# Two of the four steps that decode a 64-bit weight are rewritten from 16-bit halves to 32-bit words

## The chip, the cores and the metric

One core of one Trainium2 chip runs the kernel. The metric is the device time of one execution in microseconds. The runs of the kernel before took 761.26, 761.75 and 769.0 us, median 761.75 us.

## The reference

Three stages follow each other; the inputs of the first are float32, the weights of the other two are float64.

- Attention with a small state: x is (4, 8, 512, 64), state is (4, 8, 32, 64). `softmax(x·stateT/8)·state` gives 512 rows per batch and head, `softmax(state·xT/8)·x` gives 32 more. The result is 4·544 = 2176 tokens of 512 features.
- First MLP: `softplus(tokens @ w_in) @ w_out`, with moe_w_in 512×2048 and moe_w_out 2048×512. The weights are float64, the result is rounded to float32.
- Second MLP, with moe2_w_in, moe2_w_out (float64) and moe2_alpha: `h = x @ w_in`, `g = max(h, 0) + alpha·min(h, 0)`, `g @ w_out`, for the 2176 tokens. Digits are left out of names in the profile, so that moe_w_in stands for both MLPs' w_in.

## The kernel before, in words

**Weights.** Each of the eight quarter groups (four of each MLP, numbered g = 0 to 7) needs four chunks of w_in and four of w_out. A chunk is 128 partitions × 512 numbers of 64 bits, 512 KB. `weight_chunk` handles one: a DMA on SP's queue brings it into a staging tile (`st`, two slots in rotation; two chunks at the very start go to `stx`), seen there as 32-bit words at a step of two (8 bytes) or as 16-bit halves at a step of four. The 64-bit float is turned into a 32-bit float in four steps, all in place:

1. L268, ACT: the low word's upper half holds the bits of which three have to be moved up. A scale and a bias turn it into an integer 0 to 7, written to the low word's lower half (16 bits read, 16 bits written).
2. L270, ACT: the high word, read as a float32, times 2^-112, which leaves the exponent and mantissa bits where the shift below needs them.
3. L271, DVE: the sign bit of the high word (its upper half and 0x8000) is written to the low word's upper half.
4. L275, DVE: high word shifted left by three, or'ed with the low word. This is the float32 weight.

Then `split` (L216 on ACT, L217 on DVE) writes it as a rounded high part and a remainder, the two operands of TensorE's three passes. The remainder's subtraction is what sets the staging slot free for the next load.

**TensorE's work.** For the first 140 us or so the attention of the four batches, the products of state and w_in (`m`), and the first units of the first MLP run side by side; afterwards the work is almost only 128×512 matmuls (L226) of the two MLPs, with ACT and DVE doing the activation, the splits and the accumulation in SBUF.

**Order.** Nothing runs in the order in which it is written. Every operation is added to a graph with an engine, a price in us and the keys that it reads and writes (`G.add`). `order` then works back from the end to give each operation a due time, plays the graph forward with the prices, and emits every engine's instructions in the order that comes out. On the chip each engine runs its list in that order, and waits where the next instruction's inputs are not there. The prices of ACT are `act_us` (0.154 us + 0.714 ns per element from SBUF), those of DVE `dve_us` (0.069 us + one element per cycle of 0.96 GHz; with its second argument true, two). L268 and L270 are priced alike, L271 at the faster of DVE's rates. Where an operation's key was read or written by an earlier one, it waits for that; L271 writes the half that L268 reads, and reads the word that L270 writes.

Of the kernel before, what the change touches and what calls it, by code (L numbers as in the profile page):

```python
# [14 lines left out]
AF = mybir.ActivationFunctionType  # L15
ALU = mybir.AluOpType
# [25 lines left out]
PE, ACT, DVE, SP = "PE", "ACT", "DVE", "SP"  # L42
# [113 lines left out]
def act_us(n, psum):  # L156
    return n * 0.000714 + (0.112 if psum else 0.154)


def dve_us(n, fast=False):  # L160
    return n / (1920.0 if fast else 960.0) + 0.069
# [3 lines left out]
def attention_then_mlps_kernel(ctx: ExitStack, tc: tile.TileContext, xT, xn, st, st0, w1i, w1o, w2i, w2o, alpha, out):  # L165
    nc = tc.nc
    V, A, T = nc.vector, nc.scalar, nc.tensor
    G = Graph()
# [12 lines left out]
    def part(tag, name, dtype=F32, n=2048):  # L181
        if name not in lazy:
            lazy[name] = sb.tile([P, n], dtype, tag=tag, name=name)
        return lazy[name]
# [19 lines left out]
    def ring(name, n):  # L204
        count[name] = count.get(name, -1) + 1
        return count[name] % n
# [7 lines left out]
    def split(hi, lo, src, n, r, w, psum=False, also=()):  # L214
        k = [x + ("hi",) for x in w]
        G.add(ACT, act_us(n, psum), lambda: A.activation(now(hi), now(src), AF.Copy), r, k + [x for x in also if x not in k])  # L216
        G.add(DVE, dve_us(n), lambda: V.tensor_tensor(out=now(lo), in0=now(src), in1=now(hi), op=ALU.subtract), list(r) + k, [x + ("lo",) for x in w])  # L217
# [15 lines left out]
    def load(dst, src, w, r=(), nbytes=0):  # L233
        G.add(SP, 0.06, lambda: nc.sync.dma_start(out=now(dst), in_=now(src)), r, w, delay=2.4 + nbytes / RATE)
# [3 lines left out]
    def wi_ap(g, j):  # L238
        return WI[g % 2][j]().rearrange("p (c f) -> p c f", f=FW)

    def wo_ap(g, j):
        return WO[g % 2][j].rearrange("p (c d) -> p c d", d=DM)
# [4 lines left out]
    def wf(c):  # L247
        return WF()[:, c * FW:(c + 1) * FW]

    def weight_chunk(g):  # L250
        c = chunk[g]
        chunk[g] += 1
        gl = g % NG
        w_in, w_out = (w1i, w1o) if g < NG else (w2i, w2o)
        if c < KC:
            src, dst, key = w_in[c * P:(c + 1) * P, gl * FW:(gl + 1) * FW], [lambda j=j, c=c: wi_ap(g, j)[:, c, :] for j in range(2)], ("wi", g % 2, c)
        else:
            c -= KC
            src, dst, key = w_out[(gl * FC + c) * P:(gl * FC + c + 1) * P, :], [wo_ap(g, j)[:, c, :] for j in range(2)], ("wo", g % 2, c)
        extra = chunk[g] - 1 if g == 0 and chunk[g] > NST and chunk[g] <= KC else None  # L260
        i = ring("st", NST) if extra is None else None
        t = lambda: STG[i] if extra is None else part("m2", "stx", I64, 1024)[:, (extra - NST) * 512:(extra - NST + 1) * 512]
        floats = lambda: t().bitcast(F32).rearrange("p (f t) -> p f t", t=2)[:, :, 1]
        words = lambda: t().bitcast(U32).rearrange("p (f t) -> p f t", t=2)
        halves = lambda: t().bitcast(U16).rearrange("p (f t) -> p f t", t=4)
        q = lambda k: ("st", i, k) if extra is None else ("m", 2, extra - NST, k // 2, ("hi", "lo")[k % 2])
        load(t, src, [q(0), q(1), q(2), q(3)], nbytes=P * 4096)
        G.add(ACT, act_us(512, False), lambda: A.activation(halves()[:, :, 0], halves()[:, :, 1], AF.Copy, scale=2.0 ** -13, bias=2.0 ** -14 - 0.5),  # L268
              [q(1)], [q(0)])
        G.add(ACT, act_us(512, False), lambda: A.activation(floats(), floats(), AF.Copy, scale=2.0 ** -112), [], [q(2), q(3)])  # L270
        G.add(DVE, dve_us(512, True), lambda: V.tensor_scalar(out=halves()[:, :, 1], in0=halves()[:, :, 3], scalar1=0x8000, scalar2=None, op0=ALU.bitwise_and),  # L271
              [q(3)], [q(1)])
        whole = g == 0 and key[0] == "wi"
        fk = ("wi", 1, c, "hi")
        G.add(DVE, dve_us(512), lambda: V.scalar_tensor_tensor(out=wf(c).bitcast(U32) if whole else words()[:, :, 1], in0=words()[:, :, 1], scalar=3, in1=words()[:, :, 0],  # L275
                                                              op0=ALU.logical_shift_left, op1=ALU.bitwise_or),
              [q(0), q(1), q(2), q(3)], [fk] if whole else [q(2), q(3)])
        if whole:
            first_in.append(lambda: split(dst[0], dst[1], lambda: wf(c), 512, [fk], [key]))
        else:  # L280
            split(dst[0], dst[1], floats, 512, [q(2), q(3)], [key],
                  also=[("wi", 1, x, "hi") for x in range(KC)] if key[:2] == ("wi", 1) and g == 1 else [])
# [409 lines left out]
    def run(plan):  # L692
        units = [c for c in plan.split() if c[0] == "u"]
        n = -1
        for c in plan.split():
            if c[0] == "w":
                weight_chunk(int(c[1]))
            elif c == "m00":
                make_first_m()
            elif c[0] == "q":  # L700
                load_first(int(c[1]))
            elif c[0] == "v":
                first_in.pop(0)()
            elif c[0] == "m":
                make_m(int(c[1]), int(c[2]), "d" in c)
            elif c[0] == "t":
                load_state(int(c[1]))
            elif c[0] == "p":
                split_state(int(c[1]))
            elif c[0] == "X":  # L710
                split_x2(int(c[1]))
            elif c[0] == "n":
                load(nalpha, alpha.rearrange("(c p) -> p c", p=P), [("nalpha",)])
                G.add(DVE, 0.07, lambda: V.tensor_scalar(out=nalpha, in0=nalpha, scalar1=-1.0, scalar2=None, op0=ALU.mult), [], [("nalpha",)])
            elif c[0] == "S":
                step_s(int(c[1]))
                flush(LAG)
            elif c[0] == "u":
                b, g, fc = (int(x) for x in c[1:])
                n += 1  # L720
                step1(g, b, fc, n < FC or units[n - FC][1] != c[1], n + FC >= len(units) or units[n + FC][1] != c[1])
                flush(LAG)
            else:
                parts[int(c[1])][c[0]]()
# [4 lines left out]
    for g in range(NG, 2 * NG):  # L729
        for i in range(len(tiles)):  # L730
            for fc in range(FC):
                step2(g, i, fc)
                flush(LAG)
                if g == NG and i == 0 and fc == FC - 1:
                    for k in range(2, len(tiles)):
                        split_x2(k)
                if g + 1 < 2 * NG and i > 0 and chunk[g + 1] < 2 * KC:
                    weight_chunk(g + 1)
# [41 lines left out]
```

## Time and profile before

| | |
|---|---|
| runs | 761.26, 761.75, 769.0 us |
| profiled execution | 771.34 us, of which the span from first to last instruction is 768.5 us |
| mean granted TensorE clock | 0.987 of full |
| busy: PE, ACT, DVE | 747.2, 441.7, 415.5 us (97%, 57%, 54%) |
| L268 on ACT | 64 instructions (62 on `st`, 2 on `stx`), 84.8 us for the 62 |
| L271 on DVE | 64 instructions, 46.8 us for the 62 |

PE, PEld, ACT, DVE and SP are the five queues that the profile speaks of: matmuls, weight loads into the array, ScalarE, VectorE and the DMA issues. PE's busy share is high because matmuls are pipelined and their ends are modelled; what counts here is where it is idle. A duration is that of one instruction from start to end; on ACT the next instruction may start a little before the one ahead has ended.

### The profile page before, as it was taken

Reading aid. Unit: us, or ns where it says so; the run is one execution under the profiler, and the core shown is the slowest. Engines: PE = TensorE matmul, PEld = TensorE weight load, DVE = VectorE, ACT = ScalarE, POOL = GpSimd, SP = SyncE. Lnnn points to the kernel's source line nnn. Section 1 sums busy time; section 2 is a strip of 40 time slices with the busy share of each in tenths; the row PEclk is TensorE's granted clock in tenths of the full one; section 3 lists DMA queues with packets and bytes.
Section 4 is the critical chain, followed back from the end, with each engine's and each line's share of the span. In section 5 each row is a group of like instructions: output and inputs, shape, how many; then the busy total and the mean of one; then the engine's idle time right before and its main releaser. Section 6 shows DMA issues by size and latency. Waiting matters only on the chain.

```text
span 768.5 us, 9148 instructions
## 1 busy us (share of the span) xinstructions
PE 747.2 (97%) x3528; PEld 621.1 (81%) x3528; DVE 415.5 (54%) x693; ACT 441.7 (57%) x739; POOL 0.7 (0%) x6
## 2 busy tenths in 40 slices
PE   7988999999999999999999999999999999999996
PEld 6676788888788888888888898888988889888895
DVE  4786766666746753666682223764347643333342
ACT  5798989786646653766574435873347533333331
POOL 0000000000000000000000000000000000000000
PEclk8899999999999999999999999999999999999999
DMA  8334331136234513341120001220012000001111
GB/s 328 110 110 139 113 131 56 55 123 179 75 91 110 139 51 75 107 123 56 32 77 2 1 0 29 89 103 0 1 56 82 28 1 1 0 1 56 55 56 68
DMA packets 20383, 55.90 MB, mean 73 GB/s; under 512 B 4084, under 2 KB 4084, under 8 KB 19828
## 3 DMA queue, kind: packets, MB, share of 16 engines
q1 hardware_dynamic: 20340, 55.33, 22.9%
q8 instruction: 27, 0.44, 0.2%
q14 instruction: 16, 0.13, 0.1%
HBM read 43.00 MB, written 4.46 MB: 62 GB/s over the span
## 4 chain that ended last, share of the span: by engine, by line
PE 84%; ACT 8%; DMA 3%; DVE 3%; issue 1%; SPq 0%; ACTq 0%; DVEq 0%
PE pa L226 43%; PE ph L226 35%; PE px L226 3%; ACT st L268 3%; DMA st<-in_moe_w_in 2%; PE pa L348 1%; ACT st L270 1%; ACT xf L395 1%; PE ph L485 1%; DVE st L271 0%; ACT L501 0%; PE px L429 0%; ACT m L216 0%; DMA st<-in_moe_w_out 0%; ACT gs L216 0%
## 5 line engine op out<-in xcount | busy, mean ns | idle before, releaser
L226 PE MATMUL pa<-wo,gs 128*128 128x512 f32 x816 | 198.4, 390 | 0.0
L226 PE MATMUL pa<-gs,wo 128*128 128x512 f32 x768 | 191.6, 393 | 0.2 <-DVE xf L523 0.2
L226 PEld LDWEIGHTS pa<-wo,gs 128*128 128x128 f32 x816 | 152.1, 188 | 30.5
L226 PEld LDWEIGHTS pa<-gs,wo 128*128 128x128 f32 x768 | 143.1, 188 | 32.0 <-DVE xf L523 1.3
L226 PE MATMUL ph<-at,wi 128*128 128x512 f32 (+1 forms) x512 | 151.7, 377 | 0.0
L507 ACT ACTIVATE e<-ph 128x512 f32<-128x512 f32 (+2 forms) x80 | 42.7, 533 | 133.1 <-PE ph L226 132.9
L509 DVE SCALAR_TENSOR_TENSOR g<-u,nalpha,e 128x512 f32<-128x512 f32 (+2 forms) x80 | 53.5, 669 | 113.2 <-ACT u L508 113.1
L226 PEld LDWEIGHTS ph<-at,wi 128*128 128x128 f32 x512 | 95.5, 188 | 16.8
L226 PE MATMUL ph<-at,m 128*128 128x512 f32 x384 | 100.4, 397 | 0.5 <-ACT e L501 0.5
L268 ACT ACTIVATE st<-st 128x512 uint16<-128x512 uint16 x62 | 84.8, 1368 | 25.1 <-DMA st<-in_moe_w_in 20.2
L217 DVE TENSOR_TENSOR gs<-g,gs 128x512 fp32r<-128x512 f32 (+2 forms) x101 | 63.3, 627 | 62.5 <-ACT gs L216 48.3
L216 ACT ACTIVATE gs<-g 128x512 fp32r<-128x512 f32 (+2 forms) x101 | 59.0, 584 | 54.1 <-DVE g L509 46.4
L523 DVE TENSOR_TENSOR xf<-pa,xf 128x512 f32<-128x512 f32 x99 | 65.3, 688 | 39.0 <-PE pa L226 38.9
L226 PEld LDWEIGHTS ph<-at,m 128*128 128x128 f32 x384 | 72.3, 190 | 16.8 <-ACT e L501 1.0
L271 DVE TENSOR_SCALAR st<-st 128x512 uint16<-128x512 uint16 x62 | 46.8, 755 | 53.8 <-ACT st L270 53.7
L226 PE MATMUL ph<-m,wi 128*128 128x512 f32 (+1 forms) x192 | 71.8, 374 | 0.0
L270 ACT ACTIVATE st<-st 128x512 f32<-128x512 f32 x62 | 43.7, 704 | 0.0
L275 DVE SCALAR_TENSOR_TENSOR st<-st 128x512 uint32<-128x512 uint32 x60 | 41.5, 692 | 1.6
L508 ACT ACTIVATE u<-ph 128x512 f32<-128x512 f32 (+2 forms) x80 | 42.3, 529 | 0.0
L226 PEld LDWEIGHTS ph<-m,wi 128*128 128x128 f32 x192 | 36.0, 188 | 5.7
L216 ACT ACTIVATE wo<-st 128x512 fp32r<-128x512 f32 x32 | 21.5, 670 | 18.2 <-DVE st L275 11.1
L217 DVE TENSOR_TENSOR wo<-st,wo 128x512 fp32r<-128x512 f32 x32 | 22.1, 693 | 16.2 <-ACT wo L216 15.2
(116 smaller groups left out, 660.7 us busy)
## 6 DMA issues: line engine op xcount, KB each, us to landing
st<-in_moe_w_out SPq DMA_DIRECT2D x32, 512.0 KB, 3.3
st<-in_moe_w_in SPq DMA_DIRECT2D x30, 512.0 KB, 4.4
m<-mt SPq DMA_DIRECT2D x20, 256.0 KB, 3.7
out<-xf SPq DMA_DIRECT2D x17, 256.0 KB, 2.1
xt<-in_xT SPq DMA_DIRECT2D x6, 512.0 KB, 5.0
xf<-in_xn SPq DMA_DIRECT2D x3, 1024.0 KB, 8.7
m<-m SPq DMA_DIRECT2D x10, 256.0 KB, 3.0
stx<-in_moe_w_in SPq DMA_DIRECT2D x2, 512.0 KB, 8.1
```

Source lines behind the costliest of these rows:

```text
L216: G.add(ACT, act_us(n, psum), lambda: A.activation(now(hi), now(src), AF.Copy), r, k + [x for x in also if x not in k])
L217: G.add(DVE, dve_us(n), lambda: V.tensor_tensor(out=now(lo), in0=now(src), in1=now(hi), op=ALU.subtract), list(r) + k, [x + ("lo",) for x ...
L226: T.matmul(acc, lhs[x], rhs[y], start=first and (x, y) == (0, 0), stop=last and len(part) - 1 == k and len(part) != 2)
L268: G.add(ACT, act_us(512, False), lambda: A.activation(halves()[:, :, 0], halves()[:, :, 1], AF.Copy, scale=2.0 ** -13, bias=2.0 ** -14 - 0.5),
L270: G.add(ACT, act_us(512, False), lambda: A.activation(floats(), floats(), AF.Copy, scale=2.0 ** -112), [], [q(2), q(3)])
L271: G.add(DVE, dve_us(512, True), lambda: V.tensor_scalar(out=halves()[:, :, 1], in0=halves()[:, :, 3], scalar1=0x8000, scalar2=None, op0=AL ...
L275: G.add(DVE, dve_us(512), lambda: V.scalar_tensor_tensor(out=wf(c).bitcast(U32) if whole else words()[:, :, 1], in0=words()[:, :, 1], scal ...
L348: T.matmul(p_s[:, q, pos * 64:(pos + 1) * 64], xt(k)[:, hp, q * P:(q + 1) * P], state_of(b)[:, hp, half * 64:(half + 1) * 64], start=True, ...
L507: G.add(ACT, act_us(n, True), lambda: A.activation(e, h, AF.Relu), [hk], [ek])
L508: G.add(ACT, act_us(n, True), lambda: A.activation(u, h, AF.Relu, scale=-1.0), [hk], [uk])
L509: G.add(DVE, dve_us(n), lambda: V.scalar_tensor_tensor(out=g, in0=u, scalar=nalpha[:, c:c + 1], in1=e, op0=ALU.mult, op1=ALU.add), [ek, uk ...
L523: G.add(DVE, dve_us(512), lambda: V.tensor_tensor(out=dst, in0=src, in1=dst, op=ALU.add), [sk], [dk])
```

## The change

The first step writes its integer as a whole 32-bit word (the low word) instead of its lower half. The third step, which used to write the sign into the low word's upper half, becomes a 32-bit operation of two inputs: high word and 0x80000000, or'ed with the low word, written to the low word. Its price for the order is now that of one element per cycle. The keys follow: the first step writes both halves of the low word and reads nothing else; the third reads the high word and writes the low word.

```diff
-        G.add(ACT, act_us(512, False), lambda: A.activation(halves()[:, :, 0], halves()[:, :, 1], AF.Copy, scale=2.0 ** -13, bias=2.0 ** -14 - 0.5),
-              [q(1)], [q(0)])
+        G.add(ACT, act_us(512, False), lambda: A.activation(words()[:, :, 0], halves()[:, :, 1], AF.Copy, scale=2.0 ** -13, bias=2.0 ** -14 - 0.5),
+              [], [q(0), q(1)])
         G.add(ACT, act_us(512, False), lambda: A.activation(floats(), floats(), AF.Copy, scale=2.0 ** -112), [], [q(2), q(3)])
-        G.add(DVE, dve_us(512, True), lambda: V.tensor_scalar(out=halves()[:, :, 1], in0=halves()[:, :, 3], scalar1=0x8000, scalar2=None, op0=ALU.bitwise_and),
-              [q(3)], [q(1)])
+        G.add(DVE, dve_us(512), lambda: V.scalar_tensor_tensor(out=words()[:, :, 0], in0=words()[:, :, 1], scalar=0x80000000, in1=words()[:, :, 0],
+                                                              op0=ALU.bitwise_and, op1=ALU.bitwise_or),
+              [q(2), q(3)], [q(0), q(1)])
```

## Rows read from the trace of the kernel before

**Rows 1.** Busy time by stage: window, length, PE, PEld, DVE, ACT, POOL, clock, DMA, GB/s.

```profile
0.00:28.00 28.00, 22.43 (x86) 17.00 (x87) 14.11 (x24) 15.28 (x23) 0.70 (x6) 0.76 0.84 299
28.00:140.00 112.00, 103.96 (x586) 85.80 (x585) 83.11 (x169) 102.94 (x164) 0.00 (x0) 0.98 0.29 95
140.00:210.00 70.00, 69.78 (x307) 56.49 (x306) 45.13 (x69) 50.43 (x78) 0.00 (x0) 1.00 0.39 117
210.00:768.50 558.50, 551.01 (x2553) 461.81 (x2552) 273.18 (x433) 273.01 (x476) 0.00 (x0) 1.00 0.17 51
```

**Rows 2.** Chain of waits: shares by line; L268's first and last piece before 140 us.

```profile
by line: PE pa L226 42.7%; PE ph L226 34.9%; PE px L226 3.2%; ACT st L268 2.5%; DMA st<-in_moe_w_in 2.2%; issue 1.2%; PE pa L348 0.9%; ACT st L270 0.9%; ACT xf L395 0.6%; PE ph L485 0.5%; DVE st L271 0.5%; ACT L501 0.5%; PE px L429 0.5%; AC
...
8.80 1.35 ACT st L268
...
117.29 1.26 ACT st L268
```

**Rows 3.** Groups of ACT, shapes apart: xcount, busy us, mean ns, idle before, releaser.

```profile
L268 ACT ACTIVATE st<-st 128x512 uint16<-128x512 uint16 x62 | 84.8, 1368 | 25.1 <-DMA st<-in_moe_w_in 20.2 <-DMA st<-in_moe_w_out 4.8
L216 ACT ACTIVATE gs<-g 128x512 fp32r<-128x512 f32 x69 | 43.9, 636 | 34.5 <-DVE g L509 34.0
L270 ACT ACTIVATE st<-st 128x512 f32<-128x512 f32 x62 | 43.7, 704 | 0.0
```

**Rows 4.** Groups of DVE, shapes apart.

```profile
L271 DVE TENSOR_SCALAR st<-st 128x512 uint16<-128x512 uint16 x62 | 46.8, 755 | 53.8 <-ACT st L270 53.7
L275 DVE SCALAR_TENSOR_TENSOR st<-st 128x512 uint32<-128x512 uint32 x60 | 41.5, 692 | 1.6
...
L398 DVE TENSOR_SCALAR xf<-xf,small 128x512 f32<-128x512 f32 x8 | 3.8, 481 | 0.1
```

**Rows 5.** Timeline of ACT, back-to-back instructions: start, duration, instruction.

```profile
34.95 1.39 ACT L268 ACTIVATE st<-st 128x512 uint16<-128x512 uint16 x1
36.05 0.76 ACT L270 ACTIVATE st<-st 128x512 f32<-128x512 f32 x1
36.69 0.58 ACT L355 ACTIVATE xf<-px 128x512 f32<-128x512 f32 x1
```

**Rows 6.** Timeline of PE: matmuls that waited, with idle time and releaser in brackets.

```profile
9.61 1.13 PE L485 MATMUL ph<-wf,sb 128*128 128x512 f32 x2 [2.79 <-DVE wf L275]
...
46.30 1.66 PE L226 MATMUL ph<-at,m 128*128 128x512 f32 x6 [0.52 <-ACT e L501]
...
53.83 0.66 PE L416 MATMUL px<-ident,xf 128*128 128x128 f32 x4 [0.42 <-DVE at L217]
...
56.12 0.66 PE L416 MATMUL px<-ident,xf 128*128 128x128 f32 x4 [1.17 <-DVE at L217]
...
69.45 0.96 PE L226 MATMUL px<-wi,stm 128*128 128x512 f32 x3 [1.57 <-DVE m L217]
...
72.30 0.97 PE L226 MATMUL px<-wi,stm 128*128 128x512 f32 x3 [0.50 <-DVE m L217]
...
82.90 0.87 PE L384 MATMUL px<-ident,xf 128*128 128x128 f32 x6 [0.60 <-ACT xf L355]
...
102.48 2.50 PE L348 MATMUL px<-xf,xt 128*128 128x64 f32 x16 [1.02 <-DVE sr L217]
...
131.59 0.97 PE L226 MATMUL px<-wi,stm 128*128 128x512 f32 x3 [0.34 <-DVE sr L217]
...
202.97 2.62 PE L226 MATMUL pa<-gs,wo 128*128 128x512 f32 x9 [0.22 <-DVE xf L523]
```

**Rows 7.** Windows of 1 us: PE busy, granted clock, DMA share, GB/s.

```profile
11.00:12.00 1.00, 0.00 (x0) 0.82 1.02 397
12.00:13.00 1.00, 0.83 (x1) 0.50 1.08 393
...
104.00:105.00 1.00, 1.00 (x6) 0.50 0.95 385
```

**Rows 8.** Timeline of ACT: an L268 that waited for its load.

```profile
66.71 1.35 ACT L268 ACTIVATE st<-st 128x512 uint16<-128x512 uint16 x1 [1.19 <-DMA st<-in_moe_w_in]
```

## The prediction

> **What bounds the kernel now.** I read the stages first. From 140 us on PE has work in 69.78 of 70 us and in 551.01 of 558.5 us, and the missing time of the last stage is mostly the tail of the outputs; ACT and DVE have room there [rows 1]. So whatever the change saves behind 140 us stays under PE. Between 28 and 140 us it is otherwise: ACT is busy for 102.94 of 112 us, and PE is idle for 8.04 us [rows 1]. Before 28 us PE mostly waits for the first weights, with a clock of 0.76 [rows 1].
>
> Second, the chain of waits. L268 holds 2.5% of it, 19.2 us of 768.5, L270 0.9% and L271 0.5% [rows 2]. Up to 140 us the chain passes through 12 pieces of L268, first and last in [rows 2]. These are the places where a faster L268 can move the end.
>
> Third, the prices. L268 takes 1368 ns; L270 beside it, same tile, same step of 8 bytes, but whole words in and out, takes 704; contiguous words take 636 [rows 3]. L271, the DVE step on halves, takes 755, L275 on words 692 [rows 4]. Last, PE's own waits: those above 0.2 us that ACT or DVE end stand in [rows 6], but for a few small ones.
>
> **The sum is made** against the profiled execution: 771.34 us (span 768.5). It lies 9.6 us above the median of 761.75. Part of that is read from the clock: PE runs at 0.50 (1.2 of 2.4 GHz) from 12 us, after an interval from 6.8 to 12.2 us in which it ran only two matmuls, for 13 windows of 1 us, and again for some three windows around 104 us, behind the wait at 102.48 [rows 6, 7]. At full clock the first would give back at most 6.5 us and the second about 1.7, which makes 763.1, about the quick runs shown. I therefore take the saving from the profiled execution and subtract it from the median.
>
> **L268, halves to words.** No row shows ACT writing a 32-bit integer from 16-bit data. Below, the bound is 636, contiguous words; above, 1368, nothing gained; a loss I exclude, as the same 16 bits are read at the same step and L270 shows that writing whole words at that step is cheap [rows 3]. I take 704, that of L270, because tile, step and written size are those of the new form. On the chain that is not worth 0.66 us each, because ACT overlaps: behind an L268 of 1.39 us the next instruction starts after 1.10, behind an L270 of 0.76 after 0.64 [rows 5]. An L268 of 0.704 with L270's overlap of 0.12 would hold ACT for 0.58, and today's mean of 1.368 with its overlap of 0.29 holds it for 1.08; with the spread of both I take 0.51 us as the gain of a slot; only where another engine, or an ACT instruction that does not overlap, waits for L268's end is it 0.66. Twelve pieces give 6.1 us at most from ACT alone. What PE gets of it, wait by wait (the smaller of the wait and of what ACT has won on the way to it) [rows 6]:
>
> - Start, 9.61 and on: the second chunk's L268 is on the chain at 8.80 [rows 2] behind its load, which doesn't get earlier. 0.51, and 0.06 of L271: 0.57.
> - 46.30: two L268 ahead (1.02) against 0.52: 0.52. The rest is eaten by DVE, which is busy without a break ahead of this point.
> - 53.83 and 56.12: one more L268 and a small rest, 0.42 and 0.19: 0.6. Of the 1.17 us, 1.0 remains.
> - 69.45: the L268 at 66.71 waits 1.19 us for its load [rows 8], which waited for a staging slot that an earlier L268 held up. 0.51 and 0.66 for both (the next ACT instruction starts only at this L268's end): 1.2 of the 1.57 and of a small wait before it. 72.30 stays: there ACT and DVE hand `m` to each other.
> - 82.90: two L268 against 0.60: 0.6.
> - 102.48: two against 1.02: 1.02.
> - 131.59 and 202.97: 0.34 and 0.22, both gone.
>
> Sum 5.07 us. At zero I cost the other L268, three quarters of all: PE's own work hides them [rows 1]; without that cover each would give 0.51 us more.
>
> **L271, one input of halves to two inputs of words.** 692 ns, the price of L275, which has the same form (two inputs from one tile, words, 8-byte step); the other end is today's 755 [rows 4]. On the chain it has 0.5%, or 3.8 us [rows 2], some five instructions: 5×0.06 = 0.3 us, of which 0.06 is counted above; the rest is within my rounding. The one-input form on contiguous words takes 481 [rows 4], so halves at this step do not run at the fast rate now, and nothing is lost by giving it up. The Trainium skill, "VectorE: DVE Perf Modes", section "The perf-mode tier table (the rule you actually need)", speaks against the edit: a one-input operation between SBUF tiles can take two or more elements per cycle, a two-input one on 32-bit words takes one. By that rule L271 would lose 267 ns (512 elements at one instead of two per 0.96 GHz cycle, an estimate from that page), 1.3 us over five, and the saving would be 3.8. The trace disagrees for this shape: 755 against 692.
>
> **Waits and queues.** L271 now reads what L268 writes; it already had to wait for L268, whose input it overwrites, and for L270. No wait is added, and DVE's queue behind it is held no longer than now. Loads are the same 64; slots come free 0.57 us earlier per chunk, so loads start earlier, in a stage where DMA is busy 0.29 of the time [rows 1]. **The order** does change: the graph now charges L271 0.602 us for 0.336, 64 times 0.27. I cost that at nothing, since L268, L270 and L271 then run close to what the plan charges (today L268 holds ACT for 1.08 us and is charged 0.52), and bound it by the rivals below: three waits like the one at 69.45 in loss, all of PE's idle time in gain.
>
> **Forecast: 761.75 − 5.1 = 756.7 us**, with 755 to 758.5 as its own range (dip at 104 us gone; L268 at about 0.95 us). Chance 0.50.
>
> **Rivals.**
>
> *The read costs, not the write.* L268 reads halves as well as writing them, and no row parts the two. Against it: L271 reads and writes halves at 8 bytes' step and is only 63 ns above the words' price [rows 4]; but that is another engine. Then L268 stays at 1368, and only L271 gives 0.3: 761.4 us. The Trainium skill, "ScalarE: Activation LUTs", section "What ACT_TABLE_LOAD costs", bears on it: an ACTIVATE runs at one element per cycle for fp32 and bf16 alike. By that rule the written type would not matter, and the change would bring nothing on ACT; it gives 612 ns (an estimate from its figures for 512 elements), and the row of 1368 does not agree. Chance 0.15.
>
> *All of PE's waiting goes.* With ACT near its planned prices the order fits the chip, and the 8.04 us of 28 to 140 us close, with the 1.7 of clock, 0.57 and 0.22: 10.5 us, 751.2. For it: the plan charges L268 half of what it takes. Against: the handing to and fro at 72.30, and DVE at 83 of 112 us [rows 1]. Chance 0.15.
>
> *A start at half clock.* One of the three runs took 769.0, and the profile shows what such a start is. If the median of the new runs falls there: 769.0 − 5.1 = 763.9. The gap before 12 us shrinks by only 0.6 us of 4.2, so the clock may fall as before. Chance 0.12.
>
> *Slower: loads ahead of urgent work.* ACT works in order. An L268 whose load has not landed blocks what stands behind it, as at 66.71, where PE lost 1.57 us; and a wait of 1.02 was followed by low clock worth 1.7 [rows 6 to 8]. A faster ACT reaches its L268s sooner while loads take as long, and the new order may put them elsewhere. At 3.3 us a block, two outweigh the 5.1 saved; three give 766.5, four 769.7. Against it: slots come free earlier too. Chance 0.08.
>
> **How the numbers follow.** 756.7 is the likeliest case. 751 to 764 takes in the second rival up there, the unmoved time and the half-clock start, and leaves out the blocks and some of the edges. One per cent is 7.6 us, about what a measurement of this kernel can tell from no change. Faster than 754.1: the closing of all waits, 0.15, and an edge of the forecast, 0.07. Slower than 769.4: four blocks, or a half-clock start with some: 0.06. Within: 0.72.
>
> **What would show it.** L268 at 0.70 us and ACT's busy time some 42 us lower (64×0.66); L271 at 0.69; PE idle from 28 to 140 us near 3.5 instead of 8.04 us, with the waits at 46, 83 and 102 us gone and those of `m` near 72 us still there; the stages behind 140 us of the same length. Wrong: L268 near 1.37, or L268 at 0.70 with PE's idle time unchanged, its waits now ended by DVE or by DMAs.

## The result, and the profile after

The changed kernel takes 753.89 us (median of six runs, 753.45 to 759.67) against 762.64 us of six runs before. By the medians that is 8.75 us less, 1.1%. The ratio is 0.9868, with a 95% interval of 0.9828 to 0.9909, so the saving is clear of no change. Every ratio here is over the runs in the faster of two states that executions show, and is not the quotient of the medians. The profiled execution took 759.67 us, its span 757.9 against 768.5. The direction and the range held. The saving is 1.7 times the 5.1 us that were forecast: the time lies below the forecast's own 755 to 758.5, and just past the 754.1 beyond which the forecast had put a chance of 0.22.

The two lines of the decode, ACT and then DVE (groups by line, shapes apart: xcount, busy us, mean ns, idle before, releaser), beside [rows 3, 4]:

```profile
L268 ACT ACTIVATE st<-st 128x512 uint32<-128x512 uint16 x62 | 41.9, 676 | 18.3 <-DMA st<-in_moe_w_in 14.8 <-DMA st<-in_moe_w_out 3.1
L270 ACT ACTIVATE st<-st 128x512 f32<-128x512 f32 x62 | 41.2, 664 | 0.0
...
L271 DVE SCALAR_TENSOR_TENSOR st<-st 128x512 uint32<-128x512 uint32 x62 | 42.6, 689 | 29.9 <-ACT st L270 29.5
```

L268 has come down from 1368 to 676 ns, to the time of its neighbour. L271 has come from 755 to 689. The stages, with the columns of [rows 1]:

```profile
0.00:28.00 28.00, 23.30 (x88) 17.24 (x88) 14.54 (x30) 14.07 (x25) 0.70 (x6) 0.76 0.85 300
28.00:140.00 112.00, 109.58 (x629) 92.69 (x628) 85.90 (x170) 98.97 (x170) 0.00 (x0) 1.00 0.31 104
140.00:210.00 70.00, 70.00 (x308) 57.27 (x308) 44.57 (x69) 42.93 (x76) 0.00 (x0) 1.00 0.39 113
```

From 28 to 140 us PE is idle for 2.42 us, where it was 8.04, and the clock there is 1.00 where it was 0.98. The chain of waits by line:

```profile
by line: PE pa L226 45.3%; PE ph L226 36.7%; PE px L226 3.6%; PE px L430 1.4%; ACT m L216 0.9%; PE pa L349 0.9%; DMA st<-in_moe_w_in 0.8%; PE px L349 0.7%; DVE m L217 0.7%; issue 0.6%; ACT xf L396 0.5%; PE ph L486 0.5%; PE px L417 0.4%; ACT
```

L268, with 2.5% the first line behind PE in [rows 2], is gone from the head of the list, and the loads that came behind it fell from 2.2% to 0.8%. PE's waits between 28 and 140 us (timeline of PE; of the thirteen before, the larger stand in [rows 6]):

```profile
28.83 0.41 PE L373 MATMUL pa<-ident,xf 128*128 128x128 f32 x2 [0.39 <-DVE small L398]
29.49 0.85 PE L373 MATMUL pa<-ident,xf 128*128 128x128 f32 x6 [0.25 <-DVE xf L364]
...
53.79 0.66 PE L417 MATMUL px<-ident,xf 128*128 128x128 f32 x4 [1.06 <-DVE at L217]
...
72.37 2.00 PE L349 MATMUL px<-xf,xt 128*128 128x64 f32 x16 [0.18 <-DVE m L217]
...
127.07 0.97 PE L226 MATMUL px<-wi,stm 128*128 128x512 f32 x3 [0.28 <-DVE m L217]
```

The waits at 46, 69, 83 and 102 us have no counterpart; the one of 1.17 us at 56 is still there with 1.06. The one at 127 us, on `m`, is new.

### The profile page after: what moved, and what is told of

Same layout as the page of the kernel before. It is cut to its first block, busy times and chain, and to the rows that moved or that the text cites. A ratio compares the mean times of both kernels' runs of the same rounds, so it can differ in the third digit from the quotient of the medians.

```text
span 757.9 us, 9152 instructions
## 1 busy us (share of the span) xinstructions
PE 743.3 (98%) x3528; PEld 620.2 (82%) x3528; DVE 412.8 (54%) x693; ACT 406.7 (54%) x739; POOL 0.7 (0%) x6
## 4 chain that ended last, share of the span: by engine, by line
PE 91%; ACT 4%; DVE 2%; DMA 1%; issue 1%; SPq 0%; ACTq 0%
PE pa L226 45%; PE ph L226 37%; PE px L226 4%; PE px L430 1%; ACT m L216 1%; PE pa L349 1%; DMA st<-in_moe_w_in 1%; PE px L349 1%; DVE m L217 1%; ACT xf L396 1%; PE ph L486 1%; PE px L417 0%; ACT st L268 0%; ACT L502 0%; DVE xf L364 0%
## 5 line engine op out<-in xcount | busy, mean ns | idle before, releaser
L271 DVE SCALAR_TENSOR_TENSOR st<-st 128x512 uint32<-128x512 uint32 x62 | 42.6, 689 | 29.9 <-ACT st L270 29.5
L268 ACT ACTIVATE st<-st 128x512 uint32<-128x512 uint16 x62 | 41.9, 676 | 18.3 <-DMA st<-in_moe_w_in 14.8
L276 DVE SCALAR_TENSOR_TENSOR st<-st 128x512 uint32<-128x512 uint32 x60 | 41.3, 690 | 1.3
L270 ACT ACTIVATE st<-st 128x512 f32<-128x512 f32 x62 | 41.2, 664 | 0.0
```

The lines of the kernel that those rows point to most:

```text
L268: G.add(ACT, act_us(512, False), lambda: A.activation(words()[:, :, 0], halves()[:, :, 1], AF.Copy, scale=2.0 ** -13, bias=2.0 ** -14 - 0. ...
```

## The experiments

The first four kernels tell three causes apart: what is shorter on ACT, what is shorter on DVE, and the new order. All ratios are against runs of the kernel before on the same chip: median 763.87 us of 23 runs for the first four kernels, 764.61 us of 17 for the last four.

**Words in the old order.** Both steps on words; the price of L271 is the only thing that differs from the changed kernel.

```diff
-        G.add(DVE, dve_us(512), lambda: V.scalar_tensor_tensor(out=words()[:, :, 0], ...
+        G.add(DVE, dve_us(512, True), lambda: V.scalar_tensor_tensor(out=words()[:, :, 0], ...
```

> Both steps on words, but L271 priced as before, so that every engine runs its list in the order of the kernel before. Theory A (the shorter L268 is the gain): most of the 8.7 us, 754 to 756, with L268 at 0.68 us and PE idle from 28 to 140 us near 2.5 us. Theory B (the new order is the gain): L268 at 0.68 us but 759 to 762. Theory C (half and half, the forecast's 5.1 us from L268, the rest from the order): about 757.

753.6 us (752.95 to 755.49), ratio 0.9857 [0.982, 0.9895]. That is all of the gain, with the lists of PE, ACT and DVE in the sequence of the kernel before, as theory A has it. The stage from 28 to 140 us, columns as above:

```profile
28.00:140.00 112.00, 110.03 (x621) 93.59 (x620) 83.68 (x161) 98.89 (x171) 0.00 (x0) 1.00 0.32 109
```

**Halves in the new order.** The kernel before with nothing but the new price.

```diff
-        G.add(DVE, dve_us(512, True), lambda: V.tensor_scalar(out=halves()[:, :, 1], ...
+        G.add(DVE, dve_us(512), lambda: V.tensor_scalar(out=halves()[:, :, 1], ...
```

> The steps of the kernel before, on halves, but L271 priced at one element per cycle, so that every engine runs the order of the changed kernel. Theory A: 761 to 764, L268 still 1.37 us. Theory B: 754 to 757. Theory C: about 759.

767.56 us (761.11 to 771.5, 12 runs), ratio 1.0024 [0.9991, 1.0058]; L268 takes 1370 ns. The order brings no gain, and theories B and C fall. The median lies above the 761 to 764 of theory A too: 8 of the 12 runs have a mean clock of 0.990 or less, where 9 of the 23 runs before have. The quickest run, 761.11, is that of the kernel before, 761.06. Whether the new order makes such runs more frequent, 12 runs don't show.

**Words on ACT only.** The first step of the change without the third.

```diff
-        ... A.activation(halves()[:, :, 0], halves()[:, :, 1], AF.Copy, ...), [q(1)], [q(0)])
+        ... A.activation(words()[:, :, 0], halves()[:, :, 1], AF.Copy, ...), [], [q(0), q(1)])
```

> Only L268 writes a word; L271 still writes the sign as a half over the word's upper half, order as before. Theory A puts nearly all of the gain on L268: within 0.5 us of the kernel with both on words in this order. If L271 is on the chain more often than the five times that were counted: 1 to 3 us behind it.

755.6 us (753.38 to 760.37), ratio 0.9883 [0.984, 0.9926]. The median lies 2 us above that of both steps on words, which would be the 1 to 3 us of the second expectation; but three of the six runs have a mean clock of 0.993 or less. Of the runs at 0.997 or more, this kernel's three spans are 751.6 to 752.4 us, and the four with both steps on words 750.9 to 751.8. A second kernel with L271 on halves (L268 on words but for one, below) has 751.1 to 751.7 in its three. So L268 carries nearly all of the gain, and L271's share, 0 to 0.7 us by these spans, is not told apart from zero.

**Read words, write halves.** This asks which side of L268 costs, the half that it reads or the half that it writes.

```diff
-        ... A.activation(halves()[:, :, 0], halves()[:, :, 1], AF.Copy, scale=2.0 ** -13, bias=2.0 ** -14 - 0.5),
+        ... A.activation(halves()[:, :, 0], words()[:, :, 0], AF.Copy, scale=2.0 ** -29, bias=2.0 ** -14 - 0.5),
```

> L268 reads the whole low word (scale 2^-29) and writes a half as before; all else and the order as before. If the written half is what costs: L268 stays near 1.37 us and the time at 762. If it is the half that is read: L268 near 0.68 us and the time of the kernel with both steps on words in the old order. If both add: L268 near 1.0 us.

762.59 us (760.52 to 773.72, 12 runs), ratio 0.9972 [0.9937, 1.0007]. L268 in this kernel's groups:

```profile
L268 ACT ACTIVATE st<-st 128x512 uint16<-128x512 uint32 x62 | 84.7, 1366 | 22.7 <-DMA st<-in_moe_w_in 17.3 <-DMA st<-in_moe_w_out 5.3
```

1366 ns with whole words read, 676 with whole words written: it is the written half that costs, all of it.

**The second load's landing.** Where halves were written, the second chunk had landed 7.0 to 7.1 us after its issue in three profiles of three; with words 5.8 to 6.7. Two kernels cross this: halves everywhere but in the first chunk's L268, and words on ACT everywhere but there (the two tiles of the last line exchanged, and L271 on halves in both).

```diff
-        ... lambda: A.activation(halves()[:, :, 0], halves()[:, :, 1], ...
+        ... lambda one=(g == 0 and key == ('wi', 0, 0)): A.activation(words()[:, :, 0] if one else halves()[:, :, 0], halves()[:, :, 1], ...
```

> The kernel before, but the L268 of the very first chunk writes words; all other L268 and all L271 on halves, order as before. The three profiles with halves have the second chunk's load landing 7.0 to 7.1 us after its issue, the three with words 5.8 to 6.7. Theory D (an L268 on halves that runs while that load lands makes it land later): landing below 6.7 us here, and 0.5 to 1.3 us off the whole, 761 us. Theory E (chance, or something else of the change): landing at 7.0, and the time of the kernel before within 0.3 us.

> L268 on words but for the one of the very first chunk, which writes halves; L271 as before, order as before. Theory D: the second chunk's load lands 7.0 us or more after its issue and the time is 0.5 to 1.3 us above the kernel with L268 on words throughout, whose quickest runs take 753.4. Theory E: landing 5.8 to 6.7 us and the same time.

Landing of the first two loads, first in the kernel with one word, then in the one with one half:

```profile
DMA to landing us min/median/max: 4.6/5.0/5.4
```

```profile
DMA to landing us min/median/max: 4.4/5.0/5.7
```

The half-writing L268 ran while the second load was landing, and it landed after 5.7 us. Theory D had 7.0 or more there, and falls; theory E had 7.0 for the first of the two, which landed after 5.4, and that does not hold either. Over the ten profiles of this case the landing varies from 5.3 to 7.1 us, and whether that L268 writes halves does not decide it. What does stays open. The times are 765.17 us, ratio 1.0004 [0.9973, 1.0034], and 754.97 us, ratio 0.9894 [0.9842, 0.9946], its quickest run 752.89; the intervals are too wide to show or exclude the 0.5 to 1.3 us of theory D. The first of the two has another use: its profiled execution ran at full clock from 7 us to its last matmul, as did that of the words in the old order, and PE's list is the same in both, so that they can be laid side by side (next section).

**No L268 at all.** L268 emits nothing, and L271 only moves the sign.

```diff
-        ... A.activation(words()[:, :, 0], halves()[:, :, 1], AF.Copy, scale=2.0 ** -13, bias=2.0 ** -14 - 0.5),
+        ... None,
-        ... V.scalar_tensor_tensor(out=words()[:, :, 0], in0=words()[:, :, 1], scalar=0x80000000, in1=words()[:, :, 0], ...
+        ... V.tensor_scalar(out=words()[:, :, 0], in0=words()[:, :, 1], scalar1=0x80000000, scalar2=None, op0=ALU.bitwise_and),
```

> How much a faster L268 has left to give: L268 is left out, and L271 only moves the sign (one input, words), so the weights lack their three lowest bits; order as before. If ACT is still what PE waits for from 28 to 140 us, 64 slots of 0.58 us less give another 3 to 6 us, 748 to 750. If the words version has already taken what was to be had, 1 us or less: 752 to 753.

751.84 us (750.66 to 756.48), ratio 0.9841 [0.98, 0.9882]; the profile's span is 748.9 us against 750.9 with words in the old order. By the medians and these spans that is 1.8 to 2 us more, by the ratios 1.2, between the two expectations. The first 0.69 us per instruction brought about 8 us, the next 0.68 at most 2, and L271, shorter here too, may have a part in these. What is left between 28 and 140 us:

```profile
28.00:140.00 112.00, 110.97 (x624) 94.90 (x624) 79.88 (x160) 91.53 (x157) 0.00 (x0) 1.00 0.35 112
```

PE is idle for 1.03 us there. L271, on DVE, one input, whole words:

```profile
L271 DVE TENSOR_SCALAR st<-st 128x512 uint32<-128x512 uint32 x62 | 26.2, 424 | 18.7 <-ACT st L270 18.4
```

**The start kept busy.** The changed kernel with longer use of PE ahead of the first weights.

```diff
-        G.add(PE, 0.853, lambda: [T.matmul(PA[3][:, :P], ident, ident, start=True, stop=True) for _ in range(4)], [], [("pa", 3)])
+        G.add(PE, 0.853, lambda: [T.matmul(PA[3][:, :P], ident, ident, start=True, stop=True) for _ in range(7)], [], [("pa", 3)])
```

> The changed kernel with 28 instead of 16 matmuls on the identity at the start (same price in the graph, so the order is that of the changed kernel), to fill PE's idle time until the first weights are there. Expected: no fall of the clock between 11 and 25 us in any run, all runs at 753 to 754 us where now a third take 758 to 760, so a median 0 to 1 us lower. If the matmuls end after the first weights are ready, up to 1 us later.

753.66 us, all six runs between 752.83 and 754.7, ratio 0.9852 [0.9818, 0.9886]; every run has a mean clock of 0.997 or 0.998. One window of 1 us (PE busy, granted clock, DMA share, GB/s), first of the changed kernel, then of this one:

```profile
12.00:13.00 1.00, 1.00 (x3) 0.50 1.04 414
```

```profile
12.00:13.00 1.00, 1.00 (x11) 1.00 1.08 430
```

Its quickest run, 752.83, is 0.6 us below the changed kernel's 753.45, its median only 0.2; what is missing are runs like those of 758.49 and 759.67. All six runs kept their clock (0.997 or more), where 14 of 24 did in the four other kernels with L268 on words, and five of six in the one without L268: a sign that it helps, from few runs. Of the versions with full weights it is the one to keep, by the spread, not by the median.

## Why the prediction was right, and its sum too small

**L268 at 0.70 us because the write is what costs.** Right: 676 ns, and the kernel that reads words and writes halves shows the cause, which the prediction had left open with a chance of 0.15 for the read. The Trainium skill's page "ScalarE: Activation LUTs", section "What ACT_TABLE_LOAD costs", has one rate for fp32 and bf16 alike, which for 512 elements would be 612 ns (an estimate from its figures). 676 comes near that, 1366 does not.

**A slot shrinks by 0.51 us.** Right, and the prediction forgot it in its last part, where it expected 42 us less of ACT's busy time. It is 35.0 (441.7 to 406.7), near 64×0.51 = 33: overlapping instructions are counted once. In the changed kernel the next instruction starts 0.56 us behind an L268:

```profile
32.57 0.67 ACT L268 ACTIVATE st<-st 128x512 uint32<-128x512 uint16 x1
33.13 0.67 ACT L270 ACTIVATE st<-st 128x512 f32<-128x512 f32 x1
```

**What PE gets, wait by wait.** This is the term that was mis-sized. Two kernels with the same lists, both at full clock in this stretch, show it: halves but for the first L268 (span 758.1), and words in the old order (750.9), one profile of each, on different chips. The same matmuls around the wait at 46 us in [rows 6], from the timeline of PE, halves first:

```profile
37.33 0.71 PE L226 MATMUL pa<-gs,wo 128*128 128x512 f32 x2
38.55 1.65 PE L226 MATMUL ph<-at,m 128*128 128x512 f32 x6 [0.51 <-ACT e L501]
```

```profile
36.90 0.71 PE L226 MATMUL pa<-gs,wo 128*128 128x512 f32 x2
37.44 1.55 PE L226 MATMUL ph<-at,m 128*128 128x512 f32 x6
```

From one start to the next it is 1.22 us with the wait and 0.54 without. The wait cost 0.68 us, and shows 0.51. A 512-column matmul is drawn 0.39 us long, but the next one starts 0.23 behind it when nothing holds it:

```profile
132.39 0.39 PE L226 MATMUL pa<-gs,wo 128*128 128x512 f32 x1
132.62 1.54 PE L226 MATMUL ph<-at,m 128*128 128x512 f32 x6
```

A pause is seen only where it outlasts the 0.16 in between. So a wait behind such a matmul costs some 0.16 us more than its idle time, and one below 0.16 us shows none. Another 0.1 us appeared behind the restart. Start by start through both timelines:

| stretch (time in the profile before) | forecast, us | idle that went, halves | by which PE gains |
|---|---|---|---|
| start, to 36 us | 0.57 | | 0.44 |
| 46.30 | 0.52 | 0.51 | 0.77 |
| 53.83, 56.12 | 0.6 | 0.44 + 0.14 | 0.76 |
| 64 to 72.30 | 1.2 | 0.43 + 0.64 + 0.17 | 1.69 |
| 82.90 to 92 | 0.6 | 0.62 | 0.97 |
| 102.48 | 1.02 | 1.03 | 1.20 |
| near 124 | 0 | none printed | 0.35 |
| 131.59 | 0.34 | 0.37 | 0.55 |
| 202.97 | 0.22 | | 0.51 |
| sum | 5.07 | | 7.24 |

Each wait closed where the prediction said, and the two largest gains are the two that it said; the start, fifth in its list, came last. The idle time in brackets was taken for the price, and that makes the 2.2 us between the two sums: 2.0 in the rows from 46 to 131 us, 0.3 at 202.97, and 0.1 the other way at the start. Against 5.1, 8.75 us leave 3.7 to explain, so that is the larger part. The stretch near 124 us shows a wait that only this comparison finds. Halves:

```profile
113.39 1.38 PE L416 MATMUL px<-ident,xf 128*128 128x128 f32 x8
114.53 1.63 PE L226 MATMUL ph<-at,m 128*128 128x512 f32 x6
```

Words, 0.79 us from start to start in place of 1.14:

```profile
107.58 1.03 PE L416 MATMUL px<-ident,xf 128*128 128x128 f32 x8
108.37 1.64 PE L226 MATMUL ph<-at,m 128*128 128x512 f32 x6
```

**The start.** 0.57 forecast. The 1.09 us between the two profiles shown (12.17 to 11.08) are mostly the second load, which landed 0.95 us earlier, and by the two kernels that crossed it L268 does not decide that; in the pair above it landed 0.4 us later with words, and 0.44 was left.

**L271.** 0.3 us was forecast; what it brought, 0 to 0.7, is not told apart from zero. The two-input word form takes what L275 took, 689 against 692. The page "VectorE: DVE Perf Modes" of the Trainium skill, section "The perf-mode tier table (the rule you actually need)", is borne out for words by the kernel without L268: the one-input form takes 424 ns, 265 less than the two-input one at 689. It does not hold for halves at a step of 8 bytes: 755, more than the two-input form on words.

**The order costs nothing.** Right: 1.0024 with an interval around one on halves, and on words 0.9868 in the new order against 0.9857 in the old. The rival of loads ahead of urgent work did not happen; nor did "all of PE's waiting goes", since 2.42 us remain.

**The clock.** The prediction set the low clock around 104 us aside as an edge of its own range. Here it is the second thing that was missing, by the counts. Of the 40 runs of the kernel before that came with a clock, 8 have a mean of 0.997 or more; of the 24 of the four kernels with L268 on words (the one with one half among them), 14. The runs at 0.998 alone give spans of 759.3 to 760.4 us before and 751.6 to 752.3 after, some 7.9 us apart. The other 0.9 us of the medians' 8.75 fits a new kernel that loses its clock less often; it is also what the median before rose by, from 761.75 for the three runs that the forecast started from to 762.64 for six. Of the 7.9, the pair above accounts for 7.2; some 0.6 us stay open. That the wait of 1.02 us at 102.48 is what cost the clock in the middle fits: with it gone no profile of a kernel with L268 on words, or without it, shows a fall there, and the three of the kernels with every L268 on halves do. But one profile with that wait (halves but for the first L268) shows none either, so the wait is not enough by itself.

**Expected of the changed profile.** PE's idle time was expected near 3.5 us and is 2.42. The waits at 46, 83 and 102 are gone. The waits of `m` near 72 us are still there: in the old order with words, 0.33, 0.27 and 0.34; in the changed kernel only 0.18, so the new order does move these, to no effect on the whole.

## What to carry to other kernels

Price a wait of TensorE by the start-to-start time of its matmuls with and without it, not by the idle time that the trace draws: with 512 columns some 0.16 us had to be added to each here, and between 46 and 131 us waits with 4.35 us of idle time cost 6.29. Where an engine is off the bound on average, look for the stage in which it is not; here PE gained nothing more behind 203 us, where 34 of the 64 L268 run, and the same saving again was worth a quarter at most. Part a change from the order that it brings with it by changing the planner's price alone.

## What the runs showed of the hardware

- An ACT instruction that writes 16-bit halves at a step of 8 bytes takes 1366 to 1370 ns (means over 61 or 62) for 512 elements, whether it reads halves or words; writing words at that step from halves takes 674 to 676.
- On DVE the one-input form takes 755 ns on halves at a step of 8 bytes and 424 on words at that step, for 512 elements.
- The second of the first loads landed between 5.3 and 7.1 us after its issue over ten profiles; the cause is open.
- PE's clock fell to 1.2 GHz in three profiles (the kernel before, the changed one, halves in the new order) after a start in which it had only two matmuls between those on the identity and 11 to 12 us, and did not fall in two others with such a start (words on ACT only, and words read with halves written). With 28 in place of 16 matmuls on the identity the profile shows 2.4 GHz from 7 us to the last matmul, and the mean clock was 0.997 or 0.998 in all six runs.
